# Order of the last tiles of the second network: splits, output copies, stores and products

## Chip, core and metric

One core of one Trainium2 chip. The metric is device time in microseconds (us) of one execution of the whole kernel; the value quoted for a kernel is the median of its runs.

## The reference, cut to what matters

Three stages follow one another: a linear attention over 4 x 768 tokens, a first network (384 to 2048 to 384, a rational function between), and a second network (384 to 1024 to 384). Only the second network is touched:

```python
h = x @ w_in                                   # 3072 x 384 @ 384 x 1024
e = np.exp(h - h.max(-1))
sm = e / (e.sum(-1) + 1e-9)
solu = h * sm
ln = (solu - mean) / np.sqrt(var + 1e-6) * g_ln
out = ln @ w_out                               # 3072 x 1024 @ 1024 x 384
```

## The kernel before, in words

The second network works on 24 tiles of 128 tokens, in six groups of four (`B = 4`, `NCH = 6`). For tile s:

- **up(s)** (`n_up`, L709, products at L716): 18 matmuls of 512 columns on TensorE into one of three PSUM tiles.
- **chain(s)** (`n_soft`, L726, and `n_norm`): maximum on VectorE (L735), exponential on ScalarE (L736), scaling on VectorE (L739), square on ScalarE (L741), the root on ScalarE (L749, L750) with small VectorE steps between, the normalised tile (L754) and a transposition inside blocks (L756), both on VectorE, into a buffer shared by the four tiles of a group.
- **turn(c)** (`n_turn`, L761): once all four tiles of group c are there, 16 DMAs on the SP queue (L766), four for each tile, finish the transposition. Tile s lands in slot s % 6 of a buffer with six slots (`room(2, ...)`), so a turn writes over the slots of tiles that are six earlier.
- **split(s)** (`n_split`, L768): reads that slot; ScalarE makes the high part (L772), then VectorE for the tiles in `FASTS` or GpSimd for the others makes the low part (L773).
- **down(s)** (`n_down`, L776, products at L781): 24 matmuls of 384 columns, in triples of which the first two take the high part and the third the low part; the result goes to one of two PSUM tiles `op`.
- **out(s)** (`n_out`, L787): ScalarE copies `op` to one of two buffers `o` (L790), and four DMAs (L793) store it, on the SP queue; of tile 23, two go on ScalarE's queue.

Tiles 0 to 3 run up and chain inside the first network. The loop at L937 takes tiles 4 to 23: up and chain of tile s, then, if s ends a group, the splits up to `done + 3` that belong to earlier groups (L942) and the turn, then further splits, then the down and out of tile `done`. Four values of s (`SKIP`) issue no down, so `done` runs eight tiles behind s at the end. Written out from the loop, the order around the change is: tile 18, split 12, down 10; tile 19, **split 13, turn(4)**, down 11; tile 20, split 14, down 12; tile 21, split 15, down 13; tile 22, split 16, down 14; tile 23, split 17, turn(5), down 15, split 18, down 16, and so on to down 23. A scheduler that has a model of the time sets the order on each engine from that program; it keeps the program's order between a read and a write of the same bytes. `tc.issue_after(x)` adds that the instructions inside come behind x on x's engine.

Of the kernel before, what the change touches and what calls it, by code (L numbers as in the profile page):

```python
# [12 lines left out]
AF = mybir.ActivationFunctionType  # L13
# [6 lines left out]
def _view(ap, off, dims):  # L20
    return bass.AP(ap.tensor, ap.offset + off, [list(ap.ap[0])] + [list(d) for d in dims])


def _run(*gens):
    for g in gens:
        for _ in g:
            pass
# [3 lines left out]
def kernel(  # L31
# [15 lines left out]
    nc = tc.nc  # L47
    nc.scalar.preload_act_table_set("natural_log_exp_and_others")
    B, H, S, D = q.shape
# [3 lines left out]
    CH = 128  # L53
    NCH = S // CH
    NTOK = B * CH
    KT = DM // 128
    NF1 = DF1 // 128
    NF2 = DF2 // 128
# [9 lines left out]
    C_MIN = 1e-6  # L68
    B_MAX = 4096.0
    BETA = 2.0  # L70
    FASTS = (0, 20)
    GE = 80
    NA = 5
    PRE = (1, 1, 0, 0)
# [7 lines left out]
    AHEAD = 3  # L82
# [71 lines left out]
    def network(fast):  # L154
# [7 lines left out]
        if fast:  # L162
# [7 lines left out]
                out=ident, in_=ident, pattern=[[-1, 128]], compare_op=ALU.not_equal, fill=1.0, base=0, channel_multiplier=1  # L170
# [483 lines left out]
        w2 = {}  # L654
# [19 lines left out]
        x2s = {}  # L674

        def n_load(c):
            t = x2s[c] = moe_pool.tile([128, KT, 2, NTOK], F32R, name="x2", tag="xt", bufs=2)
            for kt in range(KT):
                raw = t[:, kt, 1].bitcast(F32)
                nc.sync.dma_start(out=raw, in_=x2_d[c][:, kt, :])  # L680
                nc.scalar.activation(t[:, kt, 0], raw, AF.Copy)
                nc.gpsimd.tensor_tensor(t[:, kt, 1], raw, t[:, kt, 0].bitcast(F32), ALU.subtract)
                yield
# [16 lines left out]
        def room(n, o, size):  # L700
            if n not in area:
                area[n] = moe_pool.tile([128, GW], F32R if n == 3 else F32, name=f"room{n}", tag=f"g{n}")
            return area[n][:, o:o + size]

        lnT = {}
        outs = {}
        st2 = {}

        def n_up(s):  # L709
            c, b = divmod(s, B)  # L710
            early = s < len(EARLY) or s % 3 == 0
            hp = ph2["ps" if early else ("ha", "hb")[s % 3 % 2]].tile([128, DF2], F32, name="h2", tag="h2")
            for n in range(2):
                for kt in range(KT):
                    for x, w in ((0, "ih"), (1, "ih"), (0, "il")):
                        nc.tensor.matmul(  # L716
                            hp[:, 512 * n:512 * n + 512], lhsT=x2s[c][:, kt, x, CH * b:CH * b + CH],
                            rhs=w2[w][:, kt, 512 * n:512 * n + 512],
                            start=(kt == 0 and x == 0 and w == "ih"), stop=(kt == KT - 1 and w == "il"),
                        )  # L720
            st2[s] = {"h": hp}

        def small(d):
            return (d["sm"][:, x:x + 1] for x in range(8))

        def n_soft(s):  # L726
            d = st2[s]
            hp = d["h"]
            d["sm"] = moe_pool.tile([128, 8], F32, name="sm", tag="sm", bufs=4)
            nmx, ssum, rs, ns, ssq, lv, r0, t0 = small(d)  # L730
            g = 0 if s < 2 else s % 2
            e, so = (room(g, 4 * DF2 + DF2 * x, DF2) for x in range(2))
            d["so"] = so
            jk = moe_pool.tile([128, DF2], BF16, name="jk", tag="ft", bufs=2)
            nc.vector.tensor_reduce(nmx, hp, axis=AX.X, op=ALU.max, negate=True)  # L735
            nc.scalar.activation(e, hp, AF.Exp, bias=nmx, accum_out=ssum)  # L736
            nc.vector.tensor_scalar(rs, ssum, 1e-9, None, ALU.add)
            nc.vector.reciprocal(rs, rs)
            nc.vector.scalar_tensor_tensor(so, e, rs, hp, ALU.mult, ALU.mult, accum_out=ns)  # L739
            nc.vector.tensor_scalar(ns, ns, -1.0 / DF2, None, ALU.mult)  # L740
            nc.scalar.activation(jk, so, AF.Square, bias=ns, accum_out=ssq)  # L741

        def n_norm(s):
            c, b = divmod(s, B)
            d = st2.pop(s)
            so = d["so"]
            nmx, ssum, rs, ns, ssq, lv, r0, t0 = small(d)
            nc.vector.tensor_scalar(ssq, ssq, 1.0 / DF2, 1e-6, ALU.mult, ALU.add)
            nc.scalar.activation(lv, ssq, AF.Ln)  # L749
            nc.scalar.activation(r0, lv, AF.Exp, scale=-0.5)  # L750
            nc.vector.tensor_tensor(t0, r0, r0, ALU.mult)
            nc.vector.scalar_tensor_tensor(t0, t0, -0.5, ssq, ALU.mult, ALU.mult)
            nc.vector.scalar_tensor_tensor(r0, t0, 1.5, r0, ALU.add, ALU.mult)
            nc.vector.tensor_scalar(so, so, ns, r0, ALU.add, ALU.mult)  # L754
            T = room(c % 2, 0, 4 * DF2)
            nc.vector.transpose(  # L756
                out=_view(T, 32 * b, [[128, NF2], [NF2 * 128, 4], [1, 32]]),
                in_=so.rearrange("p (m i) -> p m i", i=32),
            )

        def n_turn(c):  # L761
            T = room(c % 2, 0, 4 * DF2).rearrange("p (r x) -> p r x", r=4)
            for qq in range(4):
                L = lnT[4 * c + qq] = room(2, DF2 * ((4 * c + qq) % 6), DF2)
                for r in range(4):
                    nc.sync.dma_start(out=L[32 * r:32 * r + 32, :], in_=T[32 * qq:32 * qq + 32, r])  # L766

        def n_split(s):  # L768
            L = lnT[s]
            hi, lo = (room(3, DF2 * (3 * x + s % 3), DF2) for x in range(2))  # L770
            with tc.issue_after(outs[s - 3].ins) if s >= (NCH - 1) * B else ExitStack():
                nc.scalar.activation(hi, L, AF.Copy)  # L772
            (nc.vector if s in FASTS else nc.gpsimd).tensor_tensor(lo, L, hi.bitcast(F32), ALU.subtract)  # L773
            lnT[s] = (hi, lo)

        def n_down(s):  # L776
            hi, lo = lnT.pop(s)
            op = ph2["ps_o"].tile([128, DM], F32, name="op", tag="op")
            for f in range(NF2):
                for x, w in ((hi, "oh"), (hi, "ol"), (lo, "oh")):  # L780
                    nc.tensor.matmul(  # L781
                        op, lhsT=x[:, 128 * f:128 * f + 128], rhs=w2[w][:, f, :],
                        start=(f == 0 and x is hi and w == "oh"), stop=(f == NF2 - 1 and x is lo),
                    )
            return op

        def n_out(s, op):  # L787
            c, qq = divmod(s, 4)
            o = moe_pool.tile([128, DM], F32, name="o", tag="st", bufs=2)
            outs[s] = nc.scalar.activation(o, op, AF.Copy)  # L790
            to = out.rearrange("(b c q j) d -> c q b j d", b=B, c=NCH, q=4)[c, qq]
            for b in range(B):
                (nc.scalar if s == NCH * B - 1 and b >= 2 else nc.sync).dma_start(out=to[b], in_=o[32 * b:32 * b + 32])  # L793

        def n_tile(s):
            n_up(s)
            n_soft(s)
            n_norm(s)
# [82 lines left out]
        for u in range(NU + LAG):  # L881
            c, f = divmod(u, NF1)
# [51 lines left out]
        NS = NCH * B  # L934
        done = 0
        cut = 0
        for s in range(len(EARLY), NS):  # L937
            if s % B == 0 and 1 < s // B + 1 < NCH:
                _run(n_load(s // B + 1))
            n_tile(s)  # L940
            if s % B == B - 1:
                while cut < min(done + AHEAD, s // B * B):  # L942
                    n_split(cut)
                    cut += 1
                n_turn(s // B)
            while cut < min(done + AHEAD, (s + 1) // B * B):
                n_split(cut)
                cut += 1
            if s not in SKIP:
                n_out(done, n_down(done))  # L950
                done += 1
        while done < NS:
            while cut < min(done + AHEAD, NS):
                n_split(cut)
                cut += 1
            n_out(done, n_down(done))
            done += 1
# [6 lines left out]
    def recurrence():  # L964
# [70 lines left out]
        sb.__exit__(None, None, None)  # L1035

    network(True)
    wide = nc.values_load(flag, min_val=0, max_val=1)
    with tc.If(wide > 0):
        recurrence()  # L1040
        network(False)
# [30 lines left out]
```

## Time and profile before

| | us |
|---|---|
| median of 3 runs (777.05 to 777.84) | 777.82 |
| the profiled execution's own time | 780.1 |
| its span, first to last instruction | 778.4 |
| TensorE busy | 732.4 (94%) |
| VectorE busy | 625.8 (80%) |
| ScalarE busy | 534.4 (69%) |
| GpSimd busy | 358.6 (46%) |

Times in the rows are us from the span's start. PE is TensorE, DVE is VectorE, ACT is ScalarE, POOL is GpSimd; SPq and ACTq are instructions that only the queue of SP or ScalarE carries out, such as issuing a DMA. In brackets behind a timeline row stands the idle time of the engine before it and what ended it.

### The profile page before, as it was taken

What the parts mean: (1) busy time and instruction counts of PE and PEld (TensorE: products, weight loads), DVE (VectorE), ACT (ScalarE), POOL (GpSimd) and SP (SyncE); (2) the same over time, 40 slices, a digit from 0 to 9 for tenths busy, and PEclk for the clock granted to TensorE, in tenths of its full rate; (3) what the DMA queues carried; (4) which work ended last, traced back from release to release, by engine and by line L of the source; (5) the groups of instructions that cost most, each with busy time, mean ns of one, the idle gap of its engine ahead of it and who ended that gap; (6) DMA issues with size and microseconds to landing.
All of it is one profiled execution on the core that took longest, in us unless ns stands there. A gap on an engine that the chain in (4) does not pass through costs nothing.

```text
span 778.4 us, 13901 instructions
## 1 busy us (share of the span) xinstructions
PE 732.4 (94%) x4976; PEld 609.3 (78%) x4976; DVE 625.8 (80%) x1110; ACT 534.4 (69%) x983; POOL 358.6 (46%) x306
## 2 busy tenths in 40 slices
PE   5766998999999999999999999999999999999976
PEld 4655776788888888777787788888888888899866
DVE  5999999989899989798989866568876888787600
ACT  2245876689888887897979787888866454545621
POOL 3256786776555445354434533432153254433331
PEclk9777899999999999999999999999999999999988
DMA  7995456466746573738371341810027155254261
GB/s 171 253 274 162 104 163 157 151 141 207 159 165 136 164 163 113 153 109 209 111 175 58 118 59 34 332 41 1 5 78 192 43 144 131 61 136 93 71 148 45
DMA packets 87278, 101.74 MB, mean 131 GB/s; under 512 B 34464, under 2 KB 63136, under 8 KB 87200
## 3 DMA queue, kind: packets, MB, share of 16 engines
q1 hardware_dynamic: 87104, 100.67, 49.1%
q8 instruction: 41, 0.67, 0.4%
q14 instruction: 37, 0.30, 0.1%
q10 hardware_dynamic: 96, 0.10, 0.0%
HBM read 60.59 MB, written 27.56 MB: 113 GB/s over the span
## 4 chain that ended last, share of the span: by engine, by line
PE 49%; DVE 27%; DMA 7%; ACT 6%; SPq 5%; issue 5%; POOL 0%; ACTq 0%; DVEq 0%; POOLq 0%
PE hp L595 19%; PE x2p L641 19%; SPq L766 4%; DVE room L756 3%; PE y L445 3%; PE op L781 2%; DVE room L739 2%; DMA st<-in_moe_w_out_dram 2%; ACT jk L741 2%; DVE sm L735 2%; PE sc L421 2%; DVE room L754 2%; DMA lent<-in_moe_w_in_dram 2%; DMA room<-room 2%; PE h L716 2%
## 5 line engine op out<-in xcount | busy, mean ns | idle before, releaser
L595 PE MATMUL hp<-xt,g 128*128 128x512 f32 x864 | 222.9, 401 | 15.8 <-DVE p L619 7.6
L629 POOL TENSOR_TENSOR gl<-p,gh 128x512 fp32r<-128x512 f32 x96 | 134.3, 1399 | 205.8 <-ACT gh L628 117.8
L595 PEld LDWEIGHTS hp<-xt,g 128*128 128x128 f32 x864 | 163.2, 192 | 57.0 <-DVE p L626 9.3
L641 PE MATMUL x2p<-gh,g 128*128 128x512 f32 x576 | 196.5, 397 | 0.4 <-ACT gh L628 0.3
L641 PEld LDWEIGHTS x2p<-gh,g 128*128 128x128 f32 x576 | 108.3, 189 | 26.9 <-ACT gh L628 2.0
L641 PE MATMUL x2p<-gl,g 128*128 128x512 f32 x288 | 113.4, 394 | 0.0
L781 PE MATMUL op<-w2oh,room 128*128 128x384 f32 x384 | 103.7, 344 | 6.3 <-ACT o L790 6.1
L773 POOL TENSOR_TENSOR room<-room,room 128x1024 fp32r<-128x1024 f32 x22 | 54.0, 2458 | 107.4 <-ACT room L772 80.0
L624 DVE SCALAR_TENSOR_TENSOR w<-w,co,hp 128x512 f32<-128x512 f32 x84 | 61.9, 737 | 45.5 <-ACT hp L623 44.7
L716 PE MATMUL h<-w2ih,x 128*128 128x512 f32 x288 | 90.8, 394 | 0.0
L781 PEld LDWEIGHTS op<-w2oh,room 128*128 128x128 f32 x384 | 71.5, 191 | 8.1 <-ACT o L790 7.2
L602 ACT ACTIVATE p<-hp,co 128x512 f32<-128x512 f32 x96 | 66.1, 688 | 13.9 <-POOL gl L629 13.2
L603 ACT ACTIVATE w<-ah,co 128x512 f32<-128x512 f32 x96 | 69.4, 724 | 6.2 <-DVE hp L625 6.0
L600 ACT ACTIVATE ah<-hp 128x512 f32<-128x512 f32 x96 | 57.0, 594 | 15.6 <-PE hp L595 15.1
L621 DVE SCALAR_TENSOR_TENSOR p<-p,co,hp 128x512 f32<-128x512 f32 x84 | 61.5, 732 | 7.4 <-ACT p L602 7.1
L623 ACT ACTIVATE hp<-ah 128x512 f32<-128x512 f32 x84 | 50.2, 598 | 24.7 <-DVE p L621 23.6
L781 PE MATMUL op<-w2ol,room 128*128 128x384 f32 x192 | 65.9, 343 | 0.0
L628 ACT ACTIVATE gh<-p 128x512 fp32r<-128x512 f32 x96 | 59.9, 624 | 5.8 <-PE x2p L641 3.2
L641 PEld LDWEIGHTS x2p<-gl,g 128*128 128x128 f32 x288 | 54.5, 189 | 11.9 <-issue 0.8
L716 PEld LDWEIGHTS h<-w2ih,x 128*128 128x128 f32 x288 | 53.9, 188 | 11.8
L626 DVE SCALAR_TENSOR_TENSOR p<-p,co,hp 128x512 f32<-128x512 f32 x84 | 62.1, 740 | 1.0
L622 ACT ACTIVATE ah<-w,co 128x512 f32<-128x512 f32 x84 | 60.8, 724 | 1.1
(168 smaller groups left out, 1260.9 us busy)
## 6 DMA issues: line engine op xcount, KB each, us to landing
room<-room SPq DMA_DIRECT2D x96, 128.0 KB, 2.3
qk_d<-qk SPq DMA_DIRECT2D x10, 771.0 KB, 4.1
st<-in_moe_w_in_dram SPq DMA_DIRECT2D x13, 512.0 KB, 4.5
st<-in_moe_w_out_dram SPq DMA_DIRECT2D x16, 384.0 KB, 3.3
qks<-qk_d SPq DMA_DIRECT2D x20, 257.0 KB, 5.0
x<-x_d SPq DMA_DIRECT2D x18, 256.0 KB, 3.2
out_dram<-o SPq DMA_DIRECT2D x94, 48.0 KB, 1.6
ra<-in_alpha_dram SPq DMA_DIRECT2D x44, 96.0 KB, 2.8
```

The costliest lines, as they stand in the source:

```text
L595: last["PE", u] = nc.tensor.matmul(hp, lhsT=w[:, kt, 128 * o:128 * o + 128], rhs=xts[c][:, kt, xx, :], start=(kt == 0 and w is hi and xx = ...
L602: nc.scalar.activation(p, hp, AF.Square, bias=co[:, 7:8])
L603: nc.scalar.activation(w, ah, AF.Square, bias=co[:, 6:7])
L621: nc.vector.scalar_tensor_tensor(p, p, a1, hp, ALU.add, ALU.mult)
L622: nc.scalar.activation(ah, w, AF.Ln, bias=rest)
L624: nc.vector.scalar_tensor_tensor(w, w, rest, hp, ALU.add, ALU.mult)
L626: fin[u] = nc.vector.scalar_tensor_tensor(p, p, a0, hp, ALU.add, ALU.mult)
L628: last["ACT", u] = nc.scalar.activation(gh, p, AF.Copy)
L629: last["POOL", u] = nc.gpsimd.tensor_tensor(gl, p, gh[:].bitcast(F32), ALU.subtract)
L641: nc.tensor.matmul(x2ps[c][d], lhsT=w[:, o, 128 * d:128 * d + 128], rhs=gg, start=(f == 0 and w is hi and gg is gh), stop=(f == NF1 - 1 an ...
L716: nc.tensor.matmul(hp[:, 512 * n:512 * n + 512], lhsT=x2s[c][:, kt, x, CH * b:CH * b + CH], rhs=w2[w][:, kt, 512 * n:512 * n + 512], start ...
L781: nc.tensor.matmul(op, lhsT=x[:, 128 * f:128 * f + 128], rhs=w2[w][:, f, :], start=(f == 0 and x is hi and w == "oh"), stop=(f == NF2 - 1 ...
```

## The change

Five edits, all in the second network:

1. `FASTS` also names tiles 21, 22 and 23: their low parts are made on VectorE.
2. `TURNED = (17, 18)`: the eight stores of tiles 17 and 18 are issued on ScalarE's queue.
3. `line(s)`: each matmul of up(20) to up(23) and of down(12) to down(23) is issued behind the one traced before it, so that on TensorE these come in the program's order.
4. The loop breaks off before tile 23. Behind it stand up(23), then split 17, down 15, out 15, split 18, down 16, out 16, then the chain of tile 23 with its exponential held behind out 15's copy and its square behind out 16's copy on ScalarE, then turn(5), and the rest as before.
5. The splits ahead of a turn (L942 to L944) are gone; a split that they made is now made by the loop behind the turn. Written out from the loops, this moves split 7 behind turn(2), split 10 behind turn(3) and split 13 behind turn(4).

```diff
-    FASTS = (0, 20)
+    FASTS = (0, 20, 21, 22, 23)
+    TURNED = (17, 18)
...
+        chain2 = [None]
+
+        def line(s):
+            return tc.issue_after(chain2[0].ins) if s >= NCH * B - B else ExitStack()
...
+                        with line(s):
+                            chain2[0] = nc.tensor.matmul(
...
-        def n_soft(s):
+        def n_soft(s, behind=(None, None)):
+            hold = [tc.issue_after(x.ins) if x is not None else ExitStack() for x in behind]
...
-            nc.scalar.activation(e, hp, AF.Exp, bias=nmx, accum_out=ssum)
+            with hold[0]:
+                nc.scalar.activation(e, hp, AF.Exp, bias=nmx, accum_out=ssum)
...
-            nc.scalar.activation(jk, so, AF.Square, bias=ns, accum_out=ssq)
+            with hold[1]:
+                nc.scalar.activation(jk, so, AF.Square, bias=ns, accum_out=ssq)
...
+                    with line(s + 2 * B):
+                        chain2[0] = nc.tensor.matmul(
...
-                (nc.scalar if s == NCH * B - 1 and b >= 2 else nc.sync).dma_start(out=to[b], in_=o[32 * b:32 * b + 32])
+                (nc.scalar if s in TURNED or s == NCH * B - 1 and b >= 2 else nc.sync).dma_start(out=to[b], in_=o[32 * b:32 * b + 32])
...
+            if s == NS - 1:
+                break
             n_tile(s)
             if s % B == B - 1:
-                while cut < min(done + AHEAD, s // B * B):
-                    n_split(cut)
-                    cut += 1
                 n_turn(s // B)
             while cut < min(done + AHEAD, (s + 1) // B * B):
                 n_split(cut)
...
+        n_up(NS - 1)
+        behind = []
+        for _ in range(2):
+            while cut < done + AHEAD:
+                n_split(cut)
+                cut += 1
+            behind.append(done)
+            n_out(done, n_down(done))
+            done += 1
+        n_soft(NS - 1, [outs[x] for x in behind])
+        n_norm(NS - 1)
+        n_turn(NCH - 1)
```

## Rows read from the trace of the kernel before

**Rows 1.** Windows: busy time of each engine, TensorE's granted clock (PEclk), DMA share, GB/s.

```profile
707.78:712.02 4.24, 4.24 (x26) 4.24 (x25) 4.10 (x8) 2.53 (x4) 0.82 (x1) 1.00 0.00 0
712.02:716.22 4.20, 4.20 (x19) 3.38 (x19) 2.32 (x7) 1.65 (x4) 1.58 (x1) 1.00 0.85 189
...
724.66:747.10 22.44, 21.87 (x121) 20.91 (x119) 12.18 (x25) 10.30 (x20) 7.46 (x3) 1.00 0.38 90
747.10:752.82 5.72, 0.01 (x2) 0.01 (x1) 0.00 (x0) 0.55 (x2) 0.00 (x0) 0.80 0.77 177
752.82:757.40 4.58, 4.58 (x14) 4.58 (x15) 0.00 (x0) 2.33 (x3) 3.61 (x2) 0.50 0.39 101
757.40:772.10 14.70, 14.69 (x83) 14.36 (x82) 0.00 (x0) 2.42 (x4) 3.49 (x2) 1.00 0.17 42
```

**Rows 2.** The chain that ended last, its end: start, duration, what.

```profile
749.86 2.31 DMA out_dram<-o
...
752.82 19.28 PE op L781 x96
```

**Rows 3.** Timeline of SP's queue from 700 us: start, duration, what, count.

```profile
711.19 10.03 SPq L766 DMA_DIRECT2D room<-room  x16
721.32 18.27 SPq L793 DMA_DIRECT2D out_dram<-o  x19
739.77 10.04 SPq L766 DMA_DIRECT2D room<-room  x16
749.86 23.61 SPq L793 DMA_DIRECT2D out_dram<-o  x27
```

**Rows 4.** Timeline of ScalarE, single instructions.

```profile
693.64 1.06 ACT L772 ACTIVATE room<-room 128x1024 fp32r<-128x1024 f32 x1
...
731.15 1.13 ACT L736 ACTIVATE room<-h,sm 128x1024 f32<-128x1024 f32 x1 [1.55 <-DVE sm L735]
...
735.09 1.15 ACT L741 ACTIVATE jk<-room,sm 128x1024 bf16<-128x1024 f32 x1 [1.40 <-DVE sm L740]
...
743.96 1.06 ACT L772 ACTIVATE room<-room 128x1024 fp32r<-128x1024 f32 x1 [5.19 <-DMA room<-room]
752.27 0.49 ACT L790 ACTIVATE o<-op 128x384 f32<-128x384 f32 x1 [7.26 <-DMA out_dram<-o]
...
772.69 0.86 ACTq L793 DMA_DIRECT2D out_dram<-o  x2
```

**Rows 5.** Timeline of TensorE: where downs begin, and two waits.

```profile
707.78 0.34 PE L781 MATMUL op<-w2oh,room 128*128 128x384 f32 x1
...
733.74 0.45 PE L781 MATMUL op<-w2oh,room 128*128 128x384 f32 x1 [0.44 <-ACT o L790]
...
752.82 0.69 PE L781 MATMUL op<-w2oh,room 128*128 128x384 f32 x1 [5.71 <-ACT o L790]
```

**Rows 6.** Splits by line from 690 us: engine, count, duration ns min/median/max, first and last start.

```profile
L772 ACT ACTIVATE room<-room x12: 1043/1050/1061, 690.0 to 759.8; 128x1024 fp32r<-128x1024 f32 x12
...
L773 POOL TENSOR_TENSOR room<-room,room x11: 2368/2403/2662, 691.1 to 761.0; 128x1024 fp32r<-128x1024 f32 x11
...
L773 DVE TENSOR_TENSOR room<-room,room x1: 1224/1224/1224, 745.0 to 745.0; 128x1024 fp32r<-128x1024 f32 x1
```

**Rows 7.** Timeline of VectorE: the transpositions of tile 19 and of tile 23.

```profile
709.88 1.25 DVE L756 STREAM_TRANSPOSE room<-room 128x1024 f32<-128x1024 f32 x1
...
738.46 1.25 DVE L756 STREAM_TRANSPOSE room<-room 128x1024 f32<-128x1024 f32 x1
```

**Rows 8.** The last DMA of turn(4) alone, and its time from issue to landing.

```profile
L766 SPq DMA_DIRECT2D room<-room x1: 588/588/588, 720.6 to 720.6; - x1
...
DMA to landing us min/median/max: 2.5/2.5/2.5
```

**Rows 9.** Windows early in the kernel, right after TensorE had idled: columns as in rows 1.

```profile
58.03:64.48 6.45, 6.19 (x18) 4.79 (x19) 6.45 (x12) 1.75 (x4) 4.32 (x3) 0.50 0.18 61
```

More of the change, by code (lines that the diff above doesn't have):

```diff
@@ L715, in n_up @@
                     for x, w in ((0, "ih"), (1, "ih"), (0, "il")):
[L716 to L720, printed above, removed]
+                        with line(s):
+                            chain2[0] = nc.tensor.matmul(
+                                hp[:, 512 * n:512 * n + 512], lhsT=x2s[c][:, kt, x, CH * b:CH * b + CH],
+                                rhs=w2[w][:, kt, 512 * n:512 * n + 512],
+                                start=(kt == 0 and x == 0 and w == "ih"), stop=(kt == KT - 1 and w == "il"),
+                            )
             st2[s] = {"h": hp}
@@ L780, in n_down @@
                 for x, w in ((hi, "oh"), (hi, "ol"), (lo, "oh")):
[L781 to L784, printed above, removed]
+                    with line(s + 2 * B):
+                        chain2[0] = nc.tensor.matmul(
+                            op, lhsT=x[:, 128 * f:128 * f + 128], rhs=w2[w][:, f, :],
+                            start=(f == 0 and x is hi and w == "oh"), stop=(f == NF2 - 1 and x is lo),
+                        )
             return op
```

## The prediction

> **What bounds the kernel now.** I read the windows of the last stage first. Up to 747.10 us TensorE never rests: a down takes 4.24 us (24 products, 0.177 us each), an up 4.20 us, and both fill their windows at clock 1.00 [rows 1]. Ups and downs already alternate: counted back from the end, nine downs (tiles 15 to 23) follow the last up at 724.66, so the down at 707.78 is tile 13's and up(22) runs behind it, at 712.02 [rows 1, 5]. [...]
>
> [...] The copy waited 7.26 us for a store, which had landed 2.31 us after its issue at 749.86 [rows 2, 4]. SP's queue shows what held the issue: turn(5) occupies it for 10.04 us from 739.77, and 27 stores stand behind it. Of the 94 stores that the code puts on that queue (24 x 4, less two) these 27 are the last: one of tile 16 and all of tiles 17 to 23 [rows 3]. The copy of tile 18 therefore waits for a buffer of tile 16, and down 20 for the `op` tile of tile 18. Tile 20's data were not late: its high part began at 743.96, when its loads had landed, and its low part on VectorE at 745.0 [rows 4, 6].
>
> **Tail, what the edits take away.** From 724.66 to the last product's end at 772.10 pass 47.44 us. Nine downs back to back need 9 x 4.24 = 38.16. The difference, **9.3 us**, is the hole, the clock behind it and smaller waits such as the 0.44 us at 733.74 [rows 1, 5]. Can the new order have all of it?
>
> - Stores of tiles 17 and 18 on ScalarE's queue: two issues took 0.86 us there [rows 4], so a tile's four hold ScalarE for 1.7 us. The stores of 15 and 16 come ahead of turn(5), since the holds put both copies ahead of tile 23's chain. Nothing of tiles 15 to 18 then stands behind the turn. The stores of tile 19 do, but copy 21 alone needs their buffer, two downs later (8.5 us).
> - The holds: as traced, the exponential of tile 23 began at 731.15 and its square at 735.09 [rows 4]. Down 15 ends at 728.90 and down 16 at 733.14 (724.66 plus one and two downs); each with a copy of 0.49 us. Both copies would have been done, so at the old pace the holds cost nothing; at the later pace below I count them again.
> - Low parts of 21 to 23 on VectorE: 1.22 us for 2.40 us on GpSimd [rows 6]. VectorE has nothing from 747.10 on [rows 1]. No gain and no cost, as the downs are 4.24 us apart.
> - The strict line of TensorE: the order is the old one, so it costs nothing by itself. It does forbid TensorE to pass a down that waits.
>
> [...]
>
> **The removed loop, what it adds.** Six slots hold the turned tiles, and tile 19 has the slot of tile 13. Before, split 13 stood ahead of turn(4): its high part ran at 693.64, the second of the twelve splits that begin with tile 12 at 690.0 [rows 4, 6]. Now it is written behind turn(4), which fills that slot with tile 19's rows. So split 13 must wait until they have landed, and the second product of tile 13 works on tile 19's rows. (Splits 7 and 10 move too, but turns 2 and 3 write other slots: cost 0, bounded by the splits' own 1.05 and 2.40 us, hidden as their downs come later.)
>
> Step by step. Turn(4) can't start before the transposition of tile 19 ends (709.88 + 1.25 = 711.13; it starts at 711.19) [rows 3, 7]. Tile 19's DMAs are its last four; the last is issued at 720.6 and lands 2.5 us later, at 723.1 [rows 8]. High part: 1.06 us, to 724.25; low part on GpSimd, as 13 is not in `FASTS`: 2.40 us, to 726.7 [rows 6]. TensorE reaches down 13 at 707.78. It waits 16.4 us, does two products with the high part, and waits for the low part. The other 22 take 22 x 0.177 = 3.9 us at full clock.
>
> The clock: after 5.71 us idle it was at 0.50 for 4.58 us of work, after an early idle stretch for 6.45 us [rows 1, 9]. Half of that is lost: 2.3 or 3.2 us. If the two early products already count, the low stretch ends 4.58 us after 724.25, at 728.8, and 1.1 us are lost. I take 2.3, from the row with the same products. Down 13 ends at 726.7 + 3.9 + 2.3 = 732.9, not 712.02: **20.9 us late**, and because of the strict line up(22), down 14, up(23) and nine downs are all as late. Nothing else fills the hole: ScalarE and VectorE finish tiles 20 and 21 in it, which TensorE had already done, and tile 22 starts only behind down 13.
>
> The tail again, now that up(23) ends at 745.56. The exponential waits for copy 15 (one down and 0.49 us: 750.3), the square for copy 16 (754.55), both later than the data. From square to the transposition's end the old trace has 735.09 to 739.71, 4.62 us [rows 4, 7], so turn(5) starts at 759.25; the first split after it starts 4.2 us later (739.77 to 743.96), at 763.45, the low part ends at 765.75. TensorE asks for tile 20 at 745.56 + 5 x 4.24 = 766.76. That cover of 1.0 us is thin: if the high part stands behind ScalarE's stores of tile 18 (763.0 to 764.7), the low part ends at 767.0, still ahead of the third product at 767.1. Cost 0, at most 0.5.
>
> **Sum.** +20.9 - 9.3 = **+11.6 us**; the stretch after the last product is unchanged. The profiled execution of 780.1 (span 778.4) becomes 791.7 (790.0). That execution is 2.3 us above the median of 777.82, so the median becomes **789.4**. Bounds: down by 1.2 (clock), 0.2 (landing in 2.3 us, as the store [rows 2]), 0.8 (spread of the runs) and 1.2 (a VectorE step of tile 20, as long as a low part, leaves tile 19's chain), to 786.0; up by 0.9 (clock), 1.7 (four stores ahead of turn(4) on SP), 0.5 (tile 20 above), 1.1 (an exponential ahead of split 13 on ScalarE) and 1.2 (a VectorE step more ahead of the turn), to 794.8.
>
> [...]
>
> **Rivals.**
>
> 1. *The wait doesn't arise; the tail decides.* If the order of split 13 and turn(4) on the chip stays the old one, 9.3 us go: 768.5, faster. The point that decides is whether tile 13's high part runs before 707.78. For it: at 693.64 it was free to run. Against it: reads and writes of one slot keep the program's order, and the split at 743.96 waited 5.19 us for just such loads [rows 4]. Chance 0.11.
> 2. *The line doesn't hold, up(22) and up(23) run in the hole.* Then 8.4 us of the wait are filled: 781.0. The diff names exactly these ups, so 0.04, of which 0.01 would fall within 0.2%.
> 3. *The holds make turn(5) late.* With ScalarE's stores and both holds in the chain, tile 20 could miss its turn and TensorE would idle once more: the old hole and clock, 5.7 + 2.3 = 8.0 us, come back: 797.4. For it: the cover of 1.0 us. Against it: a miss would cost the overrun, not the old 10 us of queue. Chance 0.05.
>
> **How the numbers follow.** The forecast has 0.80, which the range 786.0 to 794.8 holds. Faster by over 0.2% (1.6 us, about what a measurement of this kernel can tell): rival 1, 0.11. Within: 0.01. Slower: 0.80 + 0.05 + 0.03 = 0.88.
>
> **What would show it.** Right: one idle stretch of TensorE of some 16 us ending near 724, ahead of a down, ended by ScalarE's split or its loads; then a stretch at 0.50; nine downs without a hole at the end; tile 13's high part starting behind the last DMA of turn(4). Wrong: a split of tile 13 near 694, no idle stretch near 710, or a hole ahead of down 20.

## The result and the profile after

| | before | changed |
|---|---|---|
| median, 6 runs each, us | 777.83 | 787.34 |
| lowest to highest, us | 777.05 to 779.34 | 785.06 to 790.78 |
| ratio, 95% interval | | 1.0125 [1.0092, 1.0157] |
| profiled execution's own time / span, us | 780.1 / 778.4 | 786.13 / 784.4 |
| TensorE busy, us | 732.4 (94%) | 729.3 (93%) |
| GpSimd busy, us | 358.6 (46%) | 350.7 (45%) |

The changed kernel is 9.5 us slower; 789.4 was forecast, with 786.0 to 794.8. In its code the lines of the second network stand some ten further down: up L723, turn L776, high part L782, low part L783, down L792, copy L801, store L804.

The end of the chain of waits of the changed kernel (start, duration, what) shows both halves of the forecast:

```profile
714.75 2.32 DMA room<-room
...
718.28 2.36 POOL room L783
...
720.68 6.18 PE op L792 x22
726.87 4.21 PE h L723 x18
731.08 4.24 PE op L792 x24
735.32 4.19 PE h L723 x18
739.51 38.17 PE op L792 x216
...
777.75 0.49 ACT o L801
```

The chain now runs through turn(4)'s last load, the low part of tile 13 on GpSimd and the other 22 products of down 13, then through up(22), down 14 and up(23), one after the other. Behind them stand nine downs without a hole, 216 products in 38.17 us, where the chain of before had a wait for a store and 96 products alone took 19.28 [rows 2].

TensorE's timeline of the changed kernel, from the start of up(21) to the two waits in down 13:

```profile
701.72 0.63 PE L723 MATMUL h<-w2ih,x 128*128 128x512 f32 x2
...
718.26 0.69 PE L792 MATMUL op<-w2oh,room 128*128 128x384 f32 x1 [12.17 <-ACT room L782]
...
720.68 1.01 PE L792 MATMUL op<-w2oh,room 128*128 128x384 f32 x2 [1.42 <-POOL room L783]
```

These are the only two waits of TensorE in the tail, and they are the two of the forecast: for the high part, then, two products later, for the low part. The waits of 0.44 and 5.71 us [rows 5] are gone.

SP's queue of the changed kernel, from turn(4) on:

```profile
705.11 10.23 SPq L776 DMA_DIRECT2D room<-room  x16
715.44 35.65 SPq L804 DMA_DIRECT2D out_dram<-o  x20
754.04 10.26 SPq L776 DMA_DIRECT2D room<-room  x16
764.40 14.65 SPq L804 DMA_DIRECT2D out_dram<-o  x18
```

Between the turns stand 20 stores and not 19 [rows 3]: the last store of tile 16 now goes ahead of turn(5).

ScalarE's timeline of the changed kernel, with split 13, copies 15 and 16, the exponential and the square of tile 23, and split 20:

```profile
717.15 1.06 ACT L782 ACTIVATE room<-room 128x1024 fp32r<-128x1024 f32 x1 [1.03 <-DMA room<-room]
...
744.57 0.47 ACT L801 ACTIVATE o<-op 128x384 f32<-128x384 f32 x1
744.94 1.11 ACT L745 ACTIVATE room<-h,sm 128x1024 f32<-128x1024 f32 x1
...
748.87 0.47 ACT L801 ACTIVATE o<-op 128x384 f32<-128x384 f32 x1
749.24 1.14 ACT L751 ACTIVATE jk<-room,sm 128x1024 bf16<-128x1024 f32 x1
...
758.28 1.06 ACT L782 ACTIVATE room<-room 128x1024 fp32r<-128x1024 f32 x1 [1.29 <-DMA room<-room]
```

Split 13 stood at 693.64 [rows 4]; it now starts when turn(4)'s last load has landed (714.75 + 2.32). Both holds bind: exponential and square follow right behind their copies.

### The profile page after: what moved, and what is told of

The parts are those of the page before. It is cut to its first block, busy times and chain, and to the rows that moved or that the text cites. A ratio compares the mean times of both kernels' runs of the same rounds, so it can differ in the third digit from the quotient of the medians.

```text
span 784.4 us, 13889 instructions
## 1 busy us (share of the span) xinstructions
PE 729.3 (93%) x4976; PEld 607.5 (77%) x4976; DVE 625.3 (80%) x1113; ACT 534.8 (68%) x983; POOL 350.7 (45%) x303
## 4 chain that ended last, share of the span: by engine, by line
PE 40%; DVE 33%; ACT 8%; issue 7%; SPq 6%; DMA 5%; POOL 1%; ACTq 0%; DVEq 0%; POOLq 0%
PE hp L596 13%; PE x2p L642 12%; PE op L792 6%; SPq L776 3%; PE h L723 3%; DVE w L625 3%; DVE room L766 2%; DVE hp L626 2%; PE sc L422 2%; DVE p L627 2%; DVE room L748 2%; DMA rq<-in_q_dram 2%; DVE p L622 2%; PE y L446 2%; DVE sm L743 2%
## 5 line engine op out<-in xcount | busy, mean ns | idle before, releaser
L792 PE MATMUL op<-w2oh,room 128*128 128x384 f32 x384 | 103.4, 344 | 13.6 <-ACT room L782 12.2
L783 POOL TENSOR_TENSOR room<-room,room 128x1024 fp32r<-128x1024 f32 x19 | 46.2, 2431 | 107.5 <-ACT room L782 89.5
L723 PE MATMUL h<-w2ih,x 128*128 128x512 f32 x288 | 90.9, 394 | 0.0
L792 PEld LDWEIGHTS op<-w2oh,room 128*128 128x128 f32 x384 | 71.5, 192 | 15.3 <-ACT room L782 12.6
L601 ACT ACTIVATE ah<-hp 128x512 f32<-128x512 f32 x96 | 57.0, 594 | 15.1 <-PE hp L596 14.7
L792 PE MATMUL op<-w2ol,room 128*128 128x384 f32 x192 | 65.9, 343 | 0.0
L723 PEld LDWEIGHTS h<-w2ih,x 128*128 128x128 f32 x288 | 53.9, 188 | 11.8
```

The costliest lines, as they stand in the source:

```text
L723: chain2[0] = nc.tensor.matmul(hp[:, 512 * n:512 * n + 512], lhsT=x2s[c][:, kt, x, CH * b:CH * b + CH], rhs=w2[w][:, kt, 512 * n:512 * n + ...
L792: chain2[0] = nc.tensor.matmul(op, lhsT=x[:, 128 * f:128 * f + 128], rhs=w2[w][:, f, :], start=(f == 0 and x is hi and w == "oh"), stop=(f ...
```

## The experiments

Three theories stood against each other. **Slot theory**: the loss is split 13, whose slot turn(4) fills first. **Hold theory**: holds and stores on ScalarE make tile 23 late. **Line theory**: the strict order on TensorE costs the time. Later runs ask which edit brings the tail's gain. Each experiment's ratio is to runs of the kernel before on the same chip.

### The loop put back

```diff
             if s % B == B - 1:
+                while cut < min(done + AHEAD, s // B * B):
+                    n_split(cut)
+                    cut += 1
                 n_turn(s // B)
```

> The changed kernel with the removed loop put back, so that split 13 stands ahead of turn(4) again (edit 5 undone, edits 1 to 4 kept). Slot theory (the changed kernel's loss is split 13 waiting for tile 19's loads): the idle stretch ahead of down 13 is gone, the tail keeps its gain of 9.3 us against the kernel before, so 768.5 us (767 to 770). Hold theory (the loss comes from the holds and ScalarE's stores making tile 23 late): it stays at 785 or more. Line theory (the strict order on TensorE costs the time by itself): it stays at 785 or more.

Measured: 770.06 us (before: 777.22), ratio 0.9919 [0.9881, 0.9957]. Holds, line and the stores on ScalarE are all still in it, so hold and line theory fall: neither costs the time by itself. The median lies just above the 767 to 770 expected. The end of its chain of waits:

```profile
720.50 4.20 PE h L723 x18
724.70 38.17 PE op L792 x216
```

No wait of TensorE is left from 703 us on. Against the changed kernel this one edit takes 17.3 us off (787.34 to 770.06). It beats both kernels and, unlike the changed one, computes tile 13 from tile 13's own rows.

### Tile 19's loads first

```diff
-            for qq in range(4):
+            for qq in ((3, 0, 1, 2) if c == 4 else range(4)):
```

> The changed kernel with one thing changed: turn(4) issues the four loads of tile 19 first and not last. Tile 13 is computed as in the changed kernel, from tile 19's rows. Slot theory: tile 19's slot is filled 12 issues (7.7 us) earlier, split 13 and all behind it come 7.7 us earlier: 779.6 us (778 to 781.5), the idle stretch of TensorE ahead of down 13 shrinks from 12.3 us to some 4.7. Hold and line theories: no change, 787.

Measured: 779.59 us (before: 777.22), ratio 1.0049 [1.0019, 1.0078]; 7.7 us below the changed kernel. TensorE's timeline of this run:

```profile
710.65 0.69 PE L792 MATMUL op<-w2oh,room 128*128 128x384 f32 x1 [4.45 <-ACT room L782]
...
713.63 1.01 PE L792 MATMUL op<-w2oh,room 128*128 128x384 f32 x2 [1.97 <-POOL room L783]
```

The wait fell from 12.17 to 4.45 us, by 7.7 us, as twelve issues ahead of the slot were moved behind it. This ties the wait to the filling of that one slot, not to the turn as a whole: the turn's sixteen loads are the same.

### No strict order on TensorE

```diff
-            return tc.issue_after(chain2[0].ins) if s >= NCH * B - B else ExitStack()
+            return ExitStack()
```

> The changed kernel without the strict order on TensorE (edit 3 undone). Tile 13 is computed as in the changed kernel, from tile 19's rows. In this program the ups of 21, 22 and 23 come in a row ahead of down 13. Slot theory: the wait of split 13 is the same, but 8.4 us of it are filled, so 8 to 10 us go: 778 us (776 to 781), and up to 8 us of what remains against the version with the loop put back is the hole ahead of down 13. Line theory: all of the loss goes, 768 to 770. Hold theory: 785 or more.

Measured: 778.39 us (before: 777.22), ratio 1.0018 [0.9994, 1.0043]. TensorE's timeline, the first product of down 13:

```profile
718.82 0.69 PE L792 MATMUL op<-w2oh,room 128*128 128x384 f32 x1 [4.05 <-ACT room L782]
```

Down 13 starts as late as in the changed kernel (718.26), but up(22) and up(23) have run before it. The line does not make the wait; it keeps ready work out of it, and that costs 9.0 us here (787.34 to 778.39), close to the 8.4 of two ups. That was rival 2 of the prediction; its price of 781.0 was 2.6 us too high, as it starts from the forecast's longer wait.

### The loop gone in the kernel before

```diff
             if s % B == B - 1:
-                while cut < min(done + AHEAD, s // B * B):
-                    n_split(cut)
-                    cut += 1
                 n_turn(s // B)
```

> The kernel before with edit 5 alone: the loop ahead of the turn is removed, nothing else; as in the changed kernel, tile 13's second product then works on tile 19's rows. In this program TensorE has the ups of 21, 22 and 23 in a row and the downs of 13 to 23 behind them, since no strict order holds the ups back. Slot theory: split 13 starts behind turn(4)'s last load, some 23 us later than before, but two ups (8.4 us) fill the wait, a hole of 4 to 6 us stays ahead of down 13, and the old hole of 5.7 us ahead of down 20 goes, as tile 23 is early: 777 us (774 to 781). Hold and line theories (edit 5 is harmless): 777.8 with the old trace, the hole ahead of down 20 included.

Measured: 792.30 us (before: 777.22), ratio 1.0201 [1.0155, 1.0248]; the forecast failed. TensorE's timeline shows the wait ahead of down 13 and a second large one, ahead of down 17:

```profile
719.68 0.69 PE L781 MATMUL op<-w2oh,room 128*128 128x384 f32 x1 [6.25 <-ACT room L772]
...
750.35 0.69 PE L781 MATMUL op<-w2oh,room 128*128 128x384 f32 x1 [9.12 <-ACT room L772]
```

The edit was not the changed kernel's edit 5 alone. In the kernel before, the same loop also puts split 17 ahead of turn(5), and tile 23 has the slot of tile 17, so here tile 17's second product works on tile 23's rows as well; the changed kernel's new ending writes split 17 ahead of that turn itself. The next run leaves that place alone:

```diff
-                while cut < min(done + AHEAD, s // B * B):
+                while s == NS - 1 and cut < min(done + AHEAD, s // B * B):
```

> The run with the loop gone alone held a second case that its expectation had missed: split 17 came to stand behind turn(5), which fills tile 17's slot with tile 23. Here the loop is kept ahead of turn(5), so that split 13 alone moves behind its turn, in the kernel before; tile 13's second product works on tile 19's rows. Slot theory: two ups fill 8.4 us of split 13's wait, a hole of 4 to 7 us stays ahead of down 13, none ahead of down 20, and the second wait of 9.1 us that the other run showed goes with the low clock behind it: 777 us (775 to 781). Rival (the 792 us of that run came from the changed order of TensorE): 785 or more.

Measured: 781.27 us (before: 776.97), ratio 1.0040 [1.0013, 1.0066]. The row at the first product of down 13:

```profile
723.57 0.69 PE L781 MATMUL op<-w2oh,room 128*128 128x384 f32 x1 [7.31 <-ACT room L772]
```

The wait of 9.12 us is gone and the time is 11.0 us lower, so the second slot was what the first run's expectation had missed. It is a second case of the same mechanism. The median lies just above the 775 to 781 expected, and the wait, read from an execution of 784.54 us, just above the 4 to 7.

### Which edit brings the tail's gain

Five runs, three of them with the loop put back:

```diff
-    TURNED = (17, 18)
+    TURNED = ()
```

> The changed kernel with the loop put back, but the stores of tiles 17 and 18 on SP's queue again (edit 2 undone). SP then has the stores of 17 ahead of turn(5) and those of 18 behind it. Place theory (what counts is which stores stand behind the turn, and who waits for them): turn(5) starts 0.5 to 1 us later; copy 20 waits some 2 us for tile 18's stores, but its PSUM tile is wanted only by down 22, 4 us later: 770 us (769 to 772), the same as with the loop back. If the eight stores' issue time itself were what edit 2 buys: 773.5.

Measured: 770.13 us (before: 776.97), ratio 0.9911 [0.9887, 0.9935]; no wait of TensorE in the tail. Edit 2 adds nothing beside edit 4.

```diff
-        n_soft(NS - 1, [outs[x] for x in behind])
+        n_soft(NS - 1)
```

> The changed kernel with the loop put back, without the two holds on tile 23's chain (half of edit 4 undone; the order of the program, with down 15 and 16 ahead of tile 23's chain, stays). SP's queue keeps its order, all of tile 16's stores ahead of turn(5). Place theory: 770 us (769 to 772), no hole ahead of down 20. If the holds were what keeps the hole away: 775 or more, with the old 5.7 us idle.

Measured: 770.25 us (before: 776.97), ratio 0.9905 [0.9869, 0.9940]. SP's queue of this run:

```profile
716.45 18.55 SPq L804 DMA_DIRECT2D out_dram<-o  x20
735.11 10.93 SPq L776 DMA_DIRECT2D room<-room  x16
```

All 20 stores stand ahead of turn(5) without the holds, so with edit 2 in place the holds add nothing either. Whether the program's order of downs 15 and 16 and the turn would be enough without the holds and without edit 2 was not run.

```diff
-    FASTS = (0, 20, 21, 22, 23)
+    FASTS = (0, 20)
```

> The changed kernel with the loop put back, but the low parts of tiles 21 to 23 on GpSimd again (edit 1 undone). Cover theory: the downs of the tail are 4.24 us apart and GpSimd needs 2.40 us for a low part, so nothing on TensorE waits: 770 us (769 to 772). If VectorE's 1.22 us are needed: 772 or more, with waits of TensorE on GpSimd ahead of down 21 to 23.

Measured: 770.87 us (before: 776.99), ratio 0.9912 [0.9886, 0.9938], no wait of TensorE in the tail: edit 1 is worth nothing that these runs can tell.

The kernel before with tiles 16, 17 and 18 stored by ScalarE's queue:

```diff
-                (nc.scalar if s == NCH * B - 1 and b >= 2 else nc.sync)
+                (nc.scalar if s in (16, 17, 18) or s == NCH * B - 1 and b >= 2 else nc.sync)
```

> The kernel before with one edit: the stores of tiles 16, 17 and 18 go to ScalarE's queue (edit 2 with tile 16 added, none of the others). Place theory: copy 18 no longer waits for a store of tile 16 behind turn(5), the hole ahead of down 20 goes with the clock behind it, and most of 9.3 us is gained: 769.5 us (768.5 to 771.5). If the order of the program and the holds of edit 4 are needed: 775 or more.

Measured: 772.84 us (before: 776.97), ratio 0.9930 [0.9894, 0.9966]; the hole ahead of down 20 is gone (one wait of 0.2 us is left). The median is 1.3 us above the range expected.

And with 17 and 18 alone, which is edit 2 by itself:

```diff
+                (nc.scalar if s in (17, 18) or s == NCH * B - 1 and b >= 2 else nc.sync)
```

> The kernel before with edit 2 alone: stores of tiles 17 and 18 on ScalarE's queue. Place theory: one store of tile 16 still stands behind turn(5), copy 18 waits for it as before, the hole of 5.7 us ahead of down 20 stays: 777 us (775.5 to 778.5). If the issue time taken off SP is what counts: 773.5.

Measured: 771.14 us (before: 776.99), ratio 0.9932 [0.9906, 0.9959]; this forecast failed too. ScalarE's copy of tile 18, and then SP's queue behind turn(5), in this run:

```profile
744.15 0.47 ACT L790 ACTIVATE o<-op 128x384 f32<-128x384 f32 x1
```

```profile
749.02 15.95 SPq L793 DMA_DIRECT2D out_dram<-o  x19
```

Of those 19 stores the first is tile 16's, still behind the turn, and yet copy 18 ran five microseconds before it was issued. So copy 18 doesn't use tile 16's buffer here. Copy 20 does; its row:

```profile
751.87 0.49 ACT L790 ACTIVATE o<-op 128x384 f32<-128x384 f32 x1 [1.30 <-DMA out_dram<-o]
```

Its wait ended when that store, issued at 749.02, had landed 2.8 us later. The prediction had read "two buffers" as strict turns. That the scheduler hands a copy whichever buffer it expects free first is the likely reason, and is not shown. Edit 2 alone closes the hole, and so does edit 4 without edit 2 (with edits 1 and 3 beside it); together they gain it once.

### The low part of tile 13 on VectorE

```diff
-    FASTS = (0, 20)
+    FASTS = (0, 13, 20)
```

> The kernel before with the low part of tile 13 on VectorE. In the old trace a VectorE step on one column (L752) took 2.26 us where it began while GpSimd made tile 13's low part, and 0.16 elsewhere. Port theory (a VectorE step with two inputs from SBUF that begins while GpSimd's two-input operation runs ends only with it): that step takes 0.16 us here, the low part 1.22. Rival (the step waits for ScalarE's split, which is unchanged): it stays near 2.2 us. The time stays about 777 us either way, since TensorE sets it there.

Measured: 777.35 us, a single run (before: 776.99). VectorE's timeline of this run:

```profile
693.48 0.15 DVE L752 SCALAR_TENSOR_TENSOR sm<-sm 128x1 f32<-128x1 f32 x1
...
694.59 1.22 DVE L773 TENSOR_TENSOR room<-room,room 128x1024 fp32r<-128x1024 f32 x1
```

The step that took 2.26 us takes 0.15 with ScalarE's split unchanged, so the rival falls. What that has to do with the forecast stands below.

## Why the prediction was right, and where a term was off

The terms, forecast against the profiled execution:

| term, us | forecast | measured |
|---|---|---|
| TensorE reaches down 13 | 707.78 | 705.92 (701.72 + 4.20) |
| turn(4) starts, from there | +3.4 | -0.8 |
| wait for the high part, from there | 16.4 | 12.3 (718.26 - 705.92) |
| high part to low part | 2.45 | 2.42 (718.26 to 720.68) |
| other 22 products, clock included | 6.2 | 6.18 |
| nine downs | 38.16 | 38.17 |
| change of the span | +11.6 | +6.0 |

**The removed loop.** Right: split 13 waits for turn(4), TensorE for split 13, and everything behind it in the line is late. Putting the loop back and moving four loads forward show it from two sides. Right too was the step "Tile 19's DMAs are its last four": split 13 started when the last of them had landed.

**The step that failed in size** is "Turn(4) can't start before the transposition of tile 19 ends (709.88 + 1.25 = 711.13; it starts at 711.19)". The old trace's start was taken over as it stood, with 1.2 us of play. Turn(4) came 4.2 us earlier against TensorE (from +3.4 to -0.8), and the wait was 4.1 us shorter. (The forecast's 724.25 is also 0.1 us more than its terms, 723.1 + 1.06.) Another 1.9 us of the difference is that TensorE was that much ahead in the profiled execution before the change begins to act: turn(0), ahead of all that the edits touch, already started at 582.27 for 584.17. Together, 11.6 - 4.1 - 1.9 + 0.4 (the stretch from the last copy's start to the end, 6.65 for 6.23) = 6.0. The medians differ by 9.5, as the profiled execution was 2.3 us above the median before and 1.2 below it afterwards; what the other executions spent their time on can't be read, as only one of each kernel has a trace.

Why turn(4) was earlier, two pairs of rows show. VectorE and GpSimd in the kernel before, at the same moments:

```profile
629.45 2.30 DVE L753 SCALAR_TENSOR_TENSOR sm<-sm 128x1 f32<-128x1 f32 x1
...
694.93 2.26 DVE L752 SCALAR_TENSOR_TENSOR sm<-sm 128x1 f32<-128x1 f32 x1
```

```profile
629.33 2.41 POOL L773 TENSOR_TENSOR room<-room,room 128x1024 fp32r<-128x1024 f32 x1
...
694.77 2.40 POOL L773 TENSOR_TENSOR room<-room,room 128x1024 fp32r<-128x1024 f32 x1 [1.22 <-ACT room L772]
```

The same two steps on VectorE in the changed kernel:

```profile
626.37 0.16 DVE L763 SCALAR_TENSOR_TENSOR sm<-sm 128x1 f32<-128x1 f32 x1
...
690.95 0.15 DVE L762 SCALAR_TENSOR_TENSOR sm<-sm 128x1 f32<-128x1 f32 x1
```

Before, each began just after a low part on GpSimd had begun, and ended with it (629.33 + 2.41 and 694.77 + 2.40). Afterwards neither did, which saves 2.14 + 2.11 = 4.25 us on the way to turn(4). The second is the change's own doing: the low part at 694.77 was tile 13's, which has moved. The run with that low part on VectorE confirms it. The first differs between executions: in all thirteen traces VectorE, ScalarE and GpSimd do the same work there in the same order, and four have this step. In those four GpSimd's low part just before that one starts 6.3 to 6.7 us after turn(1), in the other nine 5.4. Sorted by the two steps, the traces bear it out:

| long steps | traces | start of turn(4), from the end of up(21), us |
|---|---|---|
| both | before; stores of 16, 17 and 18 on ScalarE | +3.4; +3.1 |
| the second alone | the loop put back and its three variants; stores of 17 and 18 on ScalarE | +1.1 to +1.7 |
| the first alone | loop gone alone; loop gone at turn(4) alone | +1.4; +3.1 |
| neither | changed; tile 19 first; no strict order; low part of 13 on VectorE | -0.8 to -0.2 |

The one that does not fit, +3.1 with the first step alone, was at turn(2) already some 2 us later than the other traces with that step.

**The tail.** Nine downs back to back came true, and by the traces the tail's 9.3 us are gone. By medians the gain is smaller: 7.2 us with the loop put back (777.22 to 770.06), 6.1 to 6.8 in its three variants. The run with tile 13's low part on VectorE, which has neither long step, suggests why. There turn(5) starts 11.4 us after the last up's end (725.20), and not 15.1 as in the kernel before, and the hole ahead of down 20 is 3.35 us, not 5.71:

```profile
736.58 10.13 SPq L766 DMA_DIRECT2D room<-room  x16
```

```profile
749.91 0.69 PE L781 MATMUL op<-w2oh,room 128*128 128x384 f32 x1 [3.35 <-ACT o L790]
```

Its tail is 6.3 us longer than nine downs, against 9.3 in the trace that the forecast was read from. So the two long steps very likely sat in both terms of the sum, with opposite signs; this rests on one trace.

The cause was right only in part. The prediction wrote "The stores of 15 and 16 come ahead of turn(5), since the holds put both copies ahead of tile 23's chain"; the holds are not needed beside edit 2 (770.25 without them), nor edit 2 beside edit 4 (770.13). The other reading in two expectations, that the issue time itself counts, was 773.5: an estimate from the two issues that took 0.86 us [rows 4], so 8 x 0.43 = 3.4 us for the eight moved stores. Edit 2 alone gave 5.9 us (777.0 to 771.1), with an interval of 3.2 to 7.3 that does not exclude it. The trace speaks against it all the same: what went is the hole ahead of down 20, since copy 18 no longer waited for a store behind turn(5).

**How much was luck.** The mechanism was right and both main terms were too large. By medians edit 5 costs 17.3 us (770.06 to 787.34), where 20.9 were forecast, and the tail gives back 7.2, where 9.3 were (the kernel before had 777.22 in those runs and 777.83 beside the changed kernel). With the wait alone put right (4.1 us less) the forecast would have been 785.3, outside its own range of 786.0 to 794.8; 787.34 fell inside because the tail was overrated as well, and that was luck.

**The thin cover** ahead of down 20 held. Its high part ran at 758.28, and VectorE's row for its low part in the changed kernel is this:

```profile
759.38 1.23 DVE L783 TENSOR_TENSOR room<-room,room 128x1024 fp32r<-128x1024 f32 x1 [5.40 <-ACT room L782]
```

It ends at 760.61; counted as in the prediction, TensorE came to down 20 at 739.51 + 5 x 4.24 = 760.71, so that 0.1 us was left of the 1.0 forecast. The third product, the first that needs the low part, began at 760.90, 0.3 us behind it, and no wait arose.

**The clock.** Windows of the changed kernel over down 13, columns as in rows 1:

```profile
718.26:720.68 2.42, 1.01 (x2) 0.50 (x2) 0.57 (x1) 0.00 (x0) 2.35 (x1) 0.50 0.00 0
720.68:724.20 3.52, 3.52 (x11) 3.52 (x12) 0.00 (x0) 0.00 (x0) 0.00 (x0) 0.50 0.00 0
724.20:726.87 2.67, 2.67 (x14) 2.67 (x13) 0.00 (x0) 0.10 (x1) 0.00 (x0) 0.81 0.00 0
```

After the idle stretch of 12.17 us the granted clock was 0.50 through the two early products, the wait for the low part and the first eleven products; over the last window it was 0.81. The 22 products took 6.18 us where 3.9 (22 x 0.177, the rate at clock 1.00 [rows 1]) were due: 2.3 lost, the value taken.

**Rivals.** Rival 1 (768.5, the wait doesn't arise) is what the kernel with the loop put back became, 770.06. Rival 2 is the run without the strict order. Rival 3, a miss at down 20, did not come about, by some 0.3 us.

## What to carry to other kernels

When a step is moved past another in the program, ask which bytes the two share, not only which engine they use: a loop that looked like bookkeeping kept a read ahead of the write that reuses its slot, and a shorter ending elsewhere could not pay for it. Nor was the result the same: the changed kernel's tile 13 works on tile 19's rows. The order forced on TensorE cost nothing that shows while nothing in it waited (770.06 us with the loop put back); with the wait of 12.17 us in it, it held up all the work behind, ready or not, and that cost 9.0 us (787.34 against 778.39). A start time taken from the old trace carries the old trace's accidents, so its play should come from what the steps ahead of it waited for. One accident can stand in two terms; where their signs differ, a good total hides it.

## What the runs showed of the hardware

In the kernel before, from 550 us on, a VectorE step on a single column with two inputs took 0.12 to 0.16 us where it began while GpSimd was idle (52 steps). 14 such steps took 0.7 to 2.4 us. Each began while an operation of GpSimd with two inputs ran, and ended within 0.02 us of that operation's end (two of them in the rows above). The 31 steps on one column with one input that began during such operations took 0.11 to 0.17 us. What makes the longer steps wait, no trace shows. I had looked for GpSimd's price in its own 2.40 us and not in VectorE's small steps.
